# An attention kernel: GpSimd makes fraction and octave of VectorE's score tiles, and VectorE's cubic and last sum run on 16 bits

## The chip, the cores and the metric

The kernel runs on one core of a Trainium2 chip. The metric is the device time of one execution in microseconds; lower is better. The core's engines are TensorE (PE in the profile; its weight loads are PEld), VectorE (DVE), ScalarE (ACT), GpSimd (POOL) and SyncE (SP), which starts most of the DMAs.

## The reference

Two attention branches over the same input x (2048 tokens, width 512, 32 heads of 16) are mixed by a gate. Branch A is softmax attention; its scores are 32 heads x 2048 x 2048 exponentials, and they are nearly all of the work. Branch B is linear attention with a softmax feature map.

```python
g = sigmoid((x * gate_w).sum(-1, keepdims=True))
# A
q, k, v = heads(x @ A_wqkv)
p = softmax(einsum("bhqd,bhkd->bhqk", q, k) * 16 ** -0.5)
a = merge(einsum("bhqk,bhkd->bhqd", p, v)) @ A_wo
# B
q, k, v = heads(x @ B_wqkv)
pq, pk = q @ w_phi, k @ w_phi              # per head, 16 x 16
phi_q = concat(softmax(pq), softmax(-pq)); phi_k = concat(softmax(pk), softmax(-pk))
kv, z = einsum("bhsf,bhsd->bhfd", phi_k, v), phi_k.sum(tokens)
b = merge(phi_q @ kv / (phi_q @ z + 1e-6)) @ B_wo
return g * a + (1 - g) * b
```

## The kernel before

**Tiles.** A unit is one score tile, 128 keys x 512 queries of one head. There are 2048 of them. Four units, of four heads in four row groups of TensorE, make a pack; there are 512 packs, 16 (one for each block of 128 keys) to a group of four heads and one chunk of queries, and so 32 groups. TensorE writes scores to PSUM (L1076, `_scores`), an engine exponentiates them to SBUF, and TensorE multiplies with the values (L1203, `_values`). The denominator is a 17th column of ones in V.

**ScalarE's units.** Most units (`self.mine`) are exponentiated by ScalarE in groups of three and two tiles in turn (GROUPS), which use five PSUM banks as a ring (NRING): L1127, written to the ring ET of 25 slots. The other three banks go round among all other users (accumulators of A, projections, branch B, VectorE's scores).

**VectorE's units.** `_plan_vector` (L901) chooses the units in `self.away`: SHARES says how many for each of the 32 groups; they are spread over the places 1 to 14 of the 16 packs with an integer division. Four more are in SOON. Units are made in batches of five (NB), except FIRST (two batches of two), LAST (one of four) and an odd batch for what is left over. `_vector_batch` (L934) makes one batch:

- v_bits (L955, VectorE), one for each tile: the score in PSUM, scaled by log2(e), becomes a 32-bit fixed-point number in vt: the upper bits are the octave (the power of two), the lower ones the fraction.
- v_frac (L984, GpSimd, in `_frac`): the third byte of each 32-bit word, as a 16-bit float, to vf. In pieces of three and two tiles (PIECE = 3). In the SOON batches and the last two (TAIL) VectorE does it itself (L998).
- v_line, v_sq, v_cube (L1000 to L1002, VectorE): a cubic in the fraction, 16 bits, in vf and vu.
- v_out (L970, VectorE): the 32-bit word times 2^-17, plus the cubic, as an int16 in vu, whose bits are those of a bf16 exponential.

vt has two buffers (NVT), vf one, vu three (NVU). TensorE later takes the result as `pvx`.

**The order.** Nothing is scheduled on the chip: `Plan` holds every operation with an estimated cost, a due time (`prio`, in packs) and dependencies, and `order()` simulates the engines and writes out one fixed order for each, with semaphore waits. LEAD says how many packs ahead of its use a batch's scores are due, VPRIO, HURRY, EASE, QEASE, LEASE, OEASE and NUDGE move single due times. The names in PORT are those that share an SBUF port pair in the planner's model: a PORT operation of VectorE and an operation of GpSimd that is in PORT are never let run beside each other; each gets a dependency on the other's last one:

```python
            if o.port and e in port:
                other = port["DVE" if e == "POOL" else "POOL"]
                if other is not None:
                    o.deps.append(other)
                port[e] = o
```

TensorE's queue is in order. A `vqk` (scores of a VectorE unit) takes one of the three free banks and so waits until the bank's last user, often a v_bits, is done; the scores of ScalarE's next group stand behind it.

Branch B's work (`_b_part` L1354, keys early, queries in four parts later) and the normalisation of A (`_normed` L1249) run on VectorE in between; most of their operations are in PORT.

Of the kernel before, what the change touches and what calls it, by code (L numbers as in the profile page):

```python
# [10 lines left out]
P = 128  # L11
# [12 lines left out]
OCTAVE = 1.5 * 2.0 ** 30  # L24

# [10 lines left out]
class Job:  # L36


    def __init__(self):
        self.bank = None  # L40
        self.final = {}
        self.part = False


class Op:
    def __init__(self, eng, fn, cost, name, prio, rel, kind, lat, groups=None):
# [7 lines left out]
        self.acquire = None  # L54
        self.release = None
# [15 lines left out]
class Plan:  # L71
# [12 lines left out]
    PORT = {"v_frac", "v_line", "v_sq", "v_cube", "v_out", "gate_z", "gate_h", "gate_b", "n_den", "n_mul", "kvbd", "b_grid", "b_rest",  # L84
# [3 lines left out]
    def __init__(self):  # L88
        self.ops = []
        self.now = -1  # L90
        self.made, self.nudge = {}, {}
        self.free_banks = []
        self.loaded, self.turned = 0.0, False
        self.keep = None
        self.open = None
        self.pad = None
        self.live = False
# [41 lines left out]
    def _bank_for(self, o):  # L139

        return len(self.free_banks) > (self.keep is not None and self.keep is not o.acquire)
# [19 lines left out]
    def order(self):  # L161
# [17 lines left out]
        while left:  # L179
# [4 lines left out]
            for e in self.ENGS:  # L184
                found, limit = [], 1e9
                for o in avail[e]:
# [11 lines left out]
                    if o.acquire is not None:  # L198
                        if not self._bank_for(o):
                            continue  # L200
                        r = min(b[1] for b in self.free_banks)
                        if r > t:
                            t = r
# [85 lines left out]
            if o.acquire is not None:  # L289
                k = min(range(len(self.free_banks)), key=lambda i: self.free_banks[i][1])  # L290
# [3 lines left out]
            if o.release is not None:  # L294
                self.free_banks.append((o.release.bank, o.end + o.lat, [o]))
            if o.on_commit:
                o.on_commit(o)
# [94 lines left out]
class _Kernel:  # L392
# [5 lines left out]
    NB, NVU, LEAD = 5, 3, 13  # L398
    NVT, PIECE = 2, 3
    QDUE, VPRIO, VREL, TPRIO = 32.287, -12.758, 161.0, 1  # L400
# [9 lines left out]
    ENDS = 10  # L410
# [3 lines left out]
    REST = 53  # L414
    HURRY = (0.5, -7.6, 5.1, -6.5, 6.3, -11.8, 0, -8.0, 0, -17.8, -0.4, -1.2, -12.9, 25, 0, 8.1, 12.3, 0, 0.4, 10.0, 3.8, -1.8,
              -7.4, 0.7, 7.3, 25, 8.8, 25, 5.8, -6.9, 7.6, 3.4, -25, -14.5, 1.2, -7.3, -7.5, -20.6, -17.2, 21.6, -12.2, -4.6,
              0, 10.0, -0.9, -12.6, 11.2, -4.7, -4.7, 0.8, 0, 0, 0, 0, 0, 0, 0, 0, 0, 0)
    QEASE = (0, -10, -4.8, 6.8, 6.6, 10.5, 16, 11.0, -7.8, 7.8, -3.9, -6.4, -9.2, 10.5, 8.8, 16)
    LEASE = (-1.6, 3.6, 4.0, 0.7, -0.7, -14.9, 6.4, 16.5, -4.9, 3.4)
    OEASE = (11.6, 1.0, -4.4, 23.0, 18.8, 11.8, 17.2, 6.8, 5.3, -3.9, 1.0, 3.6, 8.7, 0, 0, 0)  # L420
    EASE = (-1.8, -6.9, 0, 0, 0, -0.2, 4.4, -4.4, 0.6, -6.3, 3.6, 0, 0, -14.4, -8.5, 1.4, -5.7, -1.4, -10.4, 0, -6.6, 5.8, 0,
              -4.2, -8.4, 7.4, -4.4, -6.5, 0, -5.6, 8.6, 2.8, -8.3, 10.0, 0, -4.3, 0, -5.7, -8.9, 0, 0, -1.5, -1.1, 5.6, 8.1,
              -3.6, 0, 7.0, -0.1, 0, 0, -4.5, -1.6, 0, 0, 4.2, 0, 0, 0, 0)
    NUDGE = {
        'b_max': {11: 3.7, 23: 22.2, 67: 10.7, 74: -19.5, 79: 13.2},
        'b_out': {3: 19.0, 11: 12.0, 17: 21.2},
        'b_part': {17: 21.2},
        'b_ratio': {2: -30.6},
        'b_rec': {8: 13.7},
        'b_slope': {6: -11.3},  # L430
        'b_square': {6: -16.5, 8: 11.6},
        'b_sum': {25: 27.1},
        'b_top': {7: -9.2, 9: 10.4},
        'bn_mul': {8: 43.5},
        'bv': {33: 6.1, 39: 10.5, 45: 19.5, 57: 8.1},
        'den': {13: 12.4},
        'kproj': {44: 0.8, 45: 6.5},
        'kproj_ev': {6: 7.4, 13: -15.7},
        'kv': {5: 11.6},
        'n_den': {9: -17.4},  # L440
        'n_mul': {10: 6.8, 14: 20.1},
        'n_rec': {3: 3.0},
        'n_t1': {20: 17.9, 26: 6.9},
        'num': {14: 12.6},
        'pq': {34: 13.8, 40: 29.9, 43: -1.4, 53: -11.9, 69: -25.9, 73: 8.8, 77: 14.1, 85: -7.9, 88: -0.9, 101: 13.5,
            120: 13.9},
        'pq_ev': {14: -22.9},
        'qproj_ev': {7: -7.8, 9: -10.7},
        'v_bits': {42: 17.3},
        'v_cube': {6: -3.1, 17: -11.8},  # L450
        'v_line': {10: 6.4, 46: -18.6},
        'vproj': {33: 3.1, 52: -14.5, 61: -3.2},
        'vproj_ev': {10: -13.3, 12: -7.6},
        'vqk': {75: 4.6, 78: -22.3, 124: 17.0, 130: -21.7, 149: 19.2, 156: 14.5},
# [440 lines left out]
    SHARES = (0, 2, 4, 6, 0, 5, 2, 8, 10, 5, 11, 10, 8, 8, 9, 12, 9, 10, 2, 9, 6, 11, 9, 14, 7, 10, 5, 13, 11, 7, 12, 9)  # L895
# [38 lines left out]
    def _vector_batch(self, number, units, due, step):  # L934
# [14 lines left out]
        parts = []  # L949
        for j, u in enumerate(units):  # L950
# [5 lines left out]
                vt[:, j, :], self._bank(job), SCALE * LOG2E * 2.0 ** 24, 2.0 ** 31,  # L956
# [6 lines left out]
        for name, cost, fn, reads, writes in self._cubic(flat(vt), flat(vf), flat(vu), n, b_vt, b_vf, b_vu):  # L963
# [6 lines left out]
        self.last_out = o = op("DVE", lambda e: e.scalar_tensor_tensor(  # L970
            out=flat(vu).bitcast(I16), in0=flat(vt), scalar=2.0 ** -17, in1=flat(vu), op0=ALU.mult, op1=ALU.add),
            self.c_dve(n), reads=[b_vt, b_vu], writes=[b_vu], name="v_out", prio=prio)
        if soon:
            self.b_bq[1][number].readers += b_vt.readers
        for j, u in enumerate(units):
            self.bits[u] = parts
            self.theirs[u] = (vu[:, j, :].bitcast(BF16), o, b_vu)

# [26 lines left out]
    def _attention(self):  # L1005
# [15 lines left out]
        a = 0  # L1021
        while a < len(self.mine):
            b = min(a + self.GROUPS[len(self.exps) % 2], len(self.mine))
# [4 lines left out]
            while len(self.pvs) < done // 4:  # L1028
                self._pv(len(self.pvs))
                if len(self.pvs) % (8 * NT) == 0:  # L1030
# [3 lines left out]
                    else:  # L1034
                        self.hooks.setdefault(int(self.Q0 + self.SQ * (4 * qc + 2)) + 10, []).append(
                            lambda qc=qc: self._out(qc))

# [55 lines left out]
    def _qk(self, a, b):  # L1093
        plan, NR = self.plan, self.NRING
        units = self.mine[a:b]

        def run(e):
            for _ in range(o.filled):
                e.matmul(self.ps[:, a % NR, :], self.kT[:, 0, 0:P], self.kT[:, 0, 0:QCH], start=True, stop=True)
            return self._scores(e, units, {u: self.ps[:, (a + k) % NR, :] for k, u in enumerate(units)})  # L1100
        k = len(self.qks)
        for x in range(a, b):
            self.in_group[x] = k
        o = plan.op("PE", run, self._wide(units[-1]), reads=self._score_bufs(units), name=f"qk{k}", prio=-1000, kind="row",
# [6 lines left out]
        o.on_commit = commit  # L1111
        o.pad = k >= 8
# [6 lines left out]
    def _exp(self, a, b):  # L1119
        plan, NR, NS = self.plan, self.NRING, self.NSLOT  # L1120
# [3 lines left out]
        for x in (a, b - 1):  # L1124
            if x >= NS:
                deps.append(self.pvs[self.mine[x - NS] // 4])
        o = plan.op("ACT", lambda e: e.activation(  # L1127
            self.ET[:, a % NS:a % NS + n, :], self.ps[:, a % NR:a % NR + n, :], ACT.Exp, scale=SCALE),
            self.c_act(512 * n), deps=deps, name=f"exp{k}", prio=self.mine[a] / 4 + 1)
        if a >= len(self.mine) - NR:  # L1130
            o.on_commit = lambda o: plan.free_banks.extend((x % NR, o.end + o.lat, [o]) for x in range(a, b))
# [561 lines left out]
```

## Time and profile before

| | |
|---|---|
| median of 3 runs | 828.64 us (828.54 to 829.0) |
| the profiled execution | 828.5 us, span 826.5 us |
| granted TensorE clock | 1.000 |
| PE / DVE / ACT / POOL busy | 789.5 / 781.7 / 816.3 / 127.4 us |
| first and last exponential group (L1127) | starts at 7.3 us and 820.3 us |
| exponential groups on ScalarE | 720 |
| v_bits on VectorE | 244 to vt and 4 (SOON) to bq |

The busy time of a group of instructions is the time in which at least one of them runs; the mean length of one is longer than its share of the busy time where neighbours overlap. "Idle before" is the time that the engine stood still just ahead of them, with what ended it. TensorE's busy time includes matmuls on zeros that the planner puts into gaps (L1212).

### The profile page before, as it was taken

The page shows a single profiled execution, that of the slowest core. Times are in us where ns is not written, and L with a number is a line of the kernel's source. Part 1 is how long each engine was busy: PE and PEld are TensorE (multiplying, and loading weights), DVE is VectorE, ACT ScalarE, POOL GpSimd, SP SyncE. Part 2 cuts the span into 40 slices and gives each one's busy share as a digit, 9 for nine tenths or more (in the row PEclk, how much of TensorE's full clock was granted, in tenths as well). Part 3 has the DMA queues.
Part 4 walks back from the last instruction along what each step waited for, and adds up shares of the span by engine and source line. Part 5 has one row for each costly group of instructions (what it writes and reads, how often), then busy time and mean ns, then how long its engine had stood idle before and what let it go on. Part 6 is the DMA issues. An engine that isn't in the chain of part 4 may idle for free.

```text
span 826.5 us, 19222 instructions
## 1 busy us (share of the span) xinstructions
PE 789.5 (96%) x8494; PEld 261.8 (32%) x8536; DVE 781.7 (95%) x1039; ACT 816.3 (99%) x725; POOL 127.4 (15%) x111
## 2 busy tenths in 40 slices
PE   9999999999999999999999999999999999999998
PEld 4323333333232222233222233222332222332344
DVE  6999999999999999999999999999999989999986
ACT  7999999999999999999999999999999999999997
POOL 3001100011012221012222011211122210122210
PEclk9999999999999999999999999999999999999999
DMA  9500000000000000030000031000320000310000
GB/s 233 177 7 8 1 5 4 1 8 3 1 8 2 1 8 1 9 71 14 2 7 1 21 59 28 12 2 6 52 39 21 2 1 21 65 27 8 2 2 27
DMA packets 49027, 19.99 MB, mean 24 GB/s; under 512 B 38704, under 2 KB 48944, under 8 KB 48944
## 3 DMA queue, kind: packets, MB, share of 16 engines
q1 hardware_dynamic: 48272, 18.58, 10.2%
q8 instruction: 66, 1.08, 0.5%
q10 hardware_dynamic: 672, 0.20, 0.1%
q14 instruction: 17, 0.14, 0.1%
HBM read 6.31 MB, written 2.10 MB: 10 GB/s over the span
## 4 chain that ended last, share of the span: by engine, by line
ACT 98%; PE 1%; DVE 0%; issue 0%
ACT ET L1127 98%; PE ps L704 0%; PE ps L786 0%; PE ps L723 0%; PE ps L1076 0%; PE ps L802 0%; DVE qT L813 0%; PE ps L1203 0%; DVE xT L735 0%; DVE xT L1641 0%; PE ps L1631 0%; DVE T L1256 0%; DVE onTA L1268 0%; DVE T L1264 0%; DVE rinv L1262 0%
## 5 line engine op out<-in xcount | busy, mean ns | idle before, releaser
L1127 ACT ACTIVATE ET<-ps 128x1536 bf16<-128x1536 f32 x720 | 814.0, 1389 | 0.6 <-PE ps L1076 0.5
L1076 PE MATMUL ps<-qT,kT 32*128 32x512 bf16 (+2 forms) x2248 | 318.8, 364 | 26.9 <-ACT ET L1127 16.7
L1212 PE MATMUL ps<-kT,zero 128*32 128x512 bf16 x2836 | 235.8, 384 | 0.1
L984 POOL TENSOR_SCALAR vf<-vt 128x1536 f16<-128x1536 uint8 (+1 forms) x96 | 118.9, 1253 | 648.4 <-DVE vu L970 350.3
L1203 PE MATMUL ps<-ET,V 128*32 128x512 bf16 (+2 forms) x1973 | 196.6, 364 | 0.7 <-ACT ET L1127 0.2
L1076 PEld LDWEIGHTS ps<-qT,kT 32*128 32x128 bf16 x2248 | 84.0, 91 | 303.3 <-ACT ET L1127 216.0
L955 DVE TENSOR_SCALAR vt<-ps 128x512 uint32<-128x512 f32 x244 | 159.0, 679 | 11.4 <-PE ps L1076 8.3
L970 DVE SCALAR_TENSOR_TENSOR vu<-vt,vu 128x2560 int16<-128x2560 uint32 (+3 forms) x51 | 137.7, 2700 | 0.5
L1212 PEld LDWEIGHTS ps<-kT,zero 128*32 128x32 bf16 x2836 | 61.8, 94 | 98.7 <-issue 77.8
L1203 PE MATMUL ps<-vu,V 128*32 128x512 bf16 (+1 forms) x275 | 90.1, 362 | 0.0
L1001 DVE TENSOR_TENSOR vf<-vf 128x2560 f16<-128x2560 f16 (+3 forms) x53 | 73.9, 1394 | 0.5
L1002 DVE TENSOR_TENSOR vu<-vu,vf 128x2560 f16<-128x2560 f16 (+3 forms) x53 | 73.8, 1393 | 0.4
L1203 PEld LDWEIGHTS ps<-ET,V 128*32 128x32 bf16 x1973 | 55.2, 95 | 58.6 <-issue 34.5
L752 PE MATMUL ps<-WB,xT 128*128 128x512 bf16 x164 | 47.9, 382 | 3.0 <-issue 1.3
L1000 DVE TENSOR_SCALAR vu<-vf 128x2560 f16<-128x2560 f16 (+3 forms) x53 | 41.0, 774 | 3.2 <-POOL vf L984 3.2
L752 PE MATMUL ps<-xT,WA 128*128 128x512 bf16 (+1 forms) x124 | 36.1, 380 | 0.4 <-DVE vt L955 0.4
L1203 PEld LDWEIGHTS ps<-vu,V 128*32 128x32 bf16 x275 | 24.6, 96 | 20.8 <-issue 13.9
L1256 DVE STREAM_TRANSPOSE T<-ps 128x512 f32<-128x512 f32 (+1 forms) x35 | 23.3, 666 | 5.1 <-PE ps L1203 4.8
L1367 DVE TENSOR_SCALAR bq<-ps 128x512 bf16<-128x512 f32 x32 | 21.3, 680 | 2.3 <-PE ps L752 2.3
L752 PEld LDWEIGHTS ps<-WB,xT 128*128 128x128 bf16 x192 | 14.1, 97 | 26.3 <-issue 14.3
L848 PE MATMUL ps<-WA,xT 128*128 128x128 bf16 x256 | 18.9, 220 | 0.2 <-issue 0.2
L1421 DVE TENSOR_TENSOR vt<-vt,brec 128x4096 bf16<-128x4096 bf16 (+1 forms) x10 | 18.6, 1859 | 0.1
(106 smaller groups left out, 424.8 us busy)
## 6 DMA issues: line engine op xcount, KB each, us to landing
qT<-qraw SPq DMA_DIRECT2D x120, 16.0 KB, 1.8
xn<-in_A_x_dram SPq DMA_DIRECT2D x3, 512.0 KB, 6.6
WB<-in_B_wqkv_dram SPq DMA_DIRECT2D x3, 512.0 KB, 5.4
out_dram<-WB SPq DMA_DIRECT2D x12, 128.0 KB, 1.8
WA<-in_A_wqkv_dram SPq DMA_DIRECT2D x3, 384.0 KB, 4.3
xn<-in_A_x_dram SPq DMA_DIRECT2D x2, 256.0 KB, 3.6
WoA<-in_A_wo_dram SPq DMA_DIRECT2D x1, 512.0 KB, 6.2
WoB<-in_B_wo_dram SPq DMA_DIRECT2D x1, 512.0 KB, 7.0
```

Source lines behind the costliest of these rows:

```text
L752: mm = op("PE", lambda e, c=c: e.matmul(self._bank(job)[:, 0:n], lhs(c), rhs(c), start=(c == 0), stop=(c == 3)), self.c_pe(n), reads=reads ...
L955: parts.append(op("DVE", lambda e, j=j, job=job: e.tensor_scalar(vt[:, j, :], self._bank(job), SCALE * LOG2E * 2.0 ** 24, 2.0 ** 31, op0=A ...
L970: self.last_out = o = op("DVE", lambda e: e.scalar_tensor_tensor(out=flat(vu).bitcast(I16), in0=flat(vt), scalar=2.0 ** -17, in1=flat(vu), ...
L984: "POOL", lambda e, a=at, n=n: e.tensor_scalar(vf[:, a:a + n, :], vt[:, a:a + n, :].bitcast(U8).rearrange("p n (q h) -> p n q h", h=4)[:, ...
L1000: lambda e: e.tensor_scalar(vu, vf, CUBE, SQUARE, op0=ALU.mult, op1=ALU.add), [b_vf], [b_vu]),
L1001: ("_sq", two, lambda e: e.tensor_tensor(vf, vf, vf, ALU.mult), [b_vf], [b_vf]),
L1002: ("_cube", two, lambda e: e.tensor_tensor(vu, vu, vf, ALU.mult), [b_vf, b_vu], [b_vu]),
L1076: ins = e.matmul(out[u][:, cols], self.kT[32 * i:32 * i + 32, cp, kt * TOK:(kt + 1) * TOK], self.qT[32 * i:32 * i + 32, s, q], start=True, ...
L1127: o = plan.op("ACT", lambda e: e.activation(self.ET[:, a % NS:a % NS + n, :], self.ps[:, a % NR:a % NR + n, :], ACT.Exp, scale=SCALE), sel ...
L1203: ins = e.matmul(self._bank(ot)[32 * i:32 * i + 32, to], self.V[:, kt, g8 // 2, v0:v0 + 32], tile[:, cols], start=first and j == 0, stop=o ...
L1212: ins = e.matmul(self._bank(ot)[32 * i:32 * i + 32, lo:QCH], self.zero[:], self.kT[:, 0, lo:QCH], start=False, stop=False, tile_position=( ...
L1256: return e.transpose(to, acc if alone else acc.rearrange("p (e b d) -> p e b d", e=2, b=8))
```

## The change

`_odd` is new and takes the place of `_frac`, `_cubic` and v_out in the batches that WHOLE marks (all but the SOON batches and the last two). In them the score is scaled so that the upper 16 bits of the word in vt are the octave and the lower 16 the fraction. GpSimd reads the lower halves and makes the fraction in vf (v_frac), and reads the upper halves and makes the int16 of the octave in vu (v_grid), both in pieces of two tiles. VectorE then computes an odd cubic, (THIRD v^2 + UNIT) v, in 16 bits, in the memory of vt itself, and v_out adds two 16-bit operands. v_grid is in PORT. Beside that, SHARES, LEAD, VPRIO, ENDS, REST and all due-time tables are new. Groups wider than three and two (WIDER) and reserved banks (`where`, `hold`, `booked`) are provided for; WIDER is all zero.

```diff
-    PORT = {"v_frac", "v_line", "v_sq", ...
+    PORT = {"v_frac", "v_grid", "v_line", "v_sq", ...
...
-    NB, NVU, LEAD = 5, 3, 13
-    NVT, PIECE = 2, 3
-    QDUE, VPRIO, VREL, TPRIO = 32.287, -12.758, 161.0, 1
+    NB, NVU, LEAD = 5, 3, 31
+    NVT, PIECE = 2, 2
+    QDUE, VPRIO, VREL, TPRIO = 32.287, -3, 161.0, 1
...
-    ENDS = 10
+    ENDS = 11
...
-    REST = 53
+    WHOLE = (1, 1, 1, ...
+    WIDER = (0, 0, 0, ...
+    LATER = 0.5
+    REST = 52
...
-    SHARES = (0, 2, 4, 6, 0, 5, 2, 8, 10, 5, 11, 10, 8, 8, 9, 12, 9, 10, 2, 9, 6, 11, 9, 14, 7, 10, 5, 13, 11, 7, 12, 9)
+    SHARES = (0, 2, 5, 4, 0, 4, 2, 10, 4, 12, 9, 9, 8, 7, 10, 15, 8, 10, 1, 8, 6, 11, 8, 13, 6, 11, 5, 13, 11, 8, 11, 11)
...
+        whole = not soon and len(self.batches) - self.TAIL > number and self.WHOLE[number]
+        scale, origin = (LOG2E * 2.0 ** 16, 127 * 2.0 ** 16) if whole else (LOG2E * 2.0 ** 24, 2.0 ** 31)
...
-                vt[:, j, :], self._bank(job), SCALE * LOG2E * 2.0 ** 24, 2.0 ** 31,
+                vt[:, j, :], self._bank(job), SCALE * scale, origin,
...
+        if whole:
+            self._odd(vt, vf, vu, n, parts, b_vt, b_vf, b_vu, prio)
...
+    def _odd(self, vt, vf, vu, n, parts, b_vt, b_vf, b_vu, prio):
+
+        halves = vt.bitcast(U16).rearrange("p n (q h) -> p n q h", h=2)
+        flat = lambda t: t.rearrange("p n q -> p (n q)")
+        power = flat(vt).bitcast(FP16)[:, 0:n]
+        v, out = flat(vf), flat(vu)
...
+        free, held, made, grid = b_vf.readers or b_vf.writers, b_vu.readers or b_vu.writers, [], []
+        for a, k in pieces:
+            made.append(self.plan.op("POOL", lambda e, a=a, k=k: e.tensor_scalar(
+                vf[:, a:a + k, :], halves[:, a:a + k, :, 0], 2.0 ** -16, SHIFT, op0=ALU.mult, op1=ALU.add),
+                0.165 + k * QCH * self.POOL, deps=[*parts[a:a + k], *free, self.last_out], name="v_frac", prio=prio))
+        for a, k in pieces:
+            grid.append(self.plan.op("POOL", lambda e, a=a, k=k: e.tensor_scalar(
+                vu[:, a:a + k, :].bitcast(I16), halves[:, a:a + k, :, 1], 128, BASE, op0=ALU.mult, op1=ALU.add),
+                0.165 + k * QCH * self.POOL, deps=[*parts[a:a + k], *held], name="v_grid", prio=prio + self.LATER))
+        b_vf.writers, b_vf.readers = made, []
+        b_vu.writers, b_vu.readers = grid, []
+        b_vt.readers += made + grid
+        two, four = 0.057 + n * 0.000525, 0.066 + n * 0.000262
+        op = lambda name, cost, fn, reads, writes: self.plan.op("DVE", fn, cost, reads=reads, writes=writes, name=name, prio=prio)
+        op("v_sq", two, lambda e: e.tensor_tensor(power, v, v, ALU.mult), [b_vf], [b_vt])
+        op("v_line", four, lambda e: e.tensor_scalar(power, power, THIRD, UNIT, op0=ALU.mult, op1=ALU.add), [b_vt], [b_vt])
+        b_vt.soon = [op("v_cube", two, lambda e: e.tensor_tensor(power, power, v, ALU.mult), [b_vt, b_vf], [b_vt])]
+        self.last_out = op("v_out", two, lambda e: e.tensor_tensor(out.bitcast(I16), out.bitcast(I16), power, ALU.add), [b_vt, b_vu], [b_vu])
```

184 lines of the change are left out of this document (122 added, 62 removed).

## The prediction

> **What bounds the kernel now.** I read the page's busy times and its chain first, then the groups by shape, the waits, the timeline of one batch, and last the groups in eight equal stretches of the span.
>
> ```profile
> PE 789.5 (96%) x8494; PEld 261.8 (32%) x8536; DVE 781.7 (95%) x1039; ACT 816.3 (99%) x725; POOL 127.4 (15%) x111
> ...
> ACT 98%; PE 1%; DVE 0%; issue 0%
> ...
> L1127 ACT ACTIVATE ET<-ps 128x1536 bf16<-128x1536 f32 x720 | 814.0, 1389 | 0.6 <-PE ps L1076 0.5
> ```
>
> The chain is ScalarE's exponentials from 8.9 us to 821.6 us, and their idle time is 0.6 us in all, 0.5 of it before the first. Around them lie 8.9 us of head, 4.9 us of tail and 2.0 us outside the span: the profiled execution took 828.5 us at a span of 826.5; the median of the runs is 828.64, 0.14 more. The two shapes of exponential, by form:
>
> ```profile
> L1127 ACT ACTIVATE ET<-ps 128x1536 bf16<-128x1536 f32 x360 | 576.5, 1601 | 0.5 <-PE ps L1076 0.5
> L1127 ACT ACTIVATE ET<-ps 128x1024 bf16<-128x1024 f32 x360 | 423.7, 1177 | 0.1
> ```
>
> They overlap, so their pace is not their length: 814.0/720 = 1.131 us a group on average, and 512 columns are 1601 - 1177 = 424 ns, so three tiles take 1.131 + 0.212 = 1.343 us of the engine and two take 0.919. One score tile more or fewer on ScalarE is about 0.45 us. The time is therefore the number of ScalarE's tiles, plus whatever ScalarE has to wait. VectorE takes 248 of the 2048 tiles; what that costs it and GpSimd (by form):
>
> ```profile
> L955 DVE TENSOR_SCALAR vt<-ps 128x512 uint32<-128x512 f32 x244 | 159.0, 679 | 11.4 <-PE ps L1076 8.3
> L970 DVE SCALAR_TENSOR_TENSOR vu<-vt,vu 128x2560 int16<-128x2560 uint32 x47 | 132.3, 2815 | 0.4
> L1001 DVE TENSOR_TENSOR vf<-vf 128x2560 f16<-128x2560 f16 x47 | 69.5, 1479 | 0.4
> L1002 DVE TENSOR_TENSOR vu<-vu,vf 128x2560 f16<-128x2560 f16 x47 | 69.5, 1479 | 0.3
> L1000 DVE TENSOR_SCALAR vu<-vf 128x2560 f16<-128x2560 f16 x47 | 38.4, 817 | 2.6 <-POOL vf L984 2.6
> ...
> L984 POOL TENSOR_SCALAR vf<-vt 128x1536 f16<-128x1536 uint8 x47 | 69.1, 1471 | 533.7 <-DVE vu L970 345.6 <-DVE bq L1438 120.5 <-DVE vt L955 67.5
> L984 POOL TENSOR_SCALAR vf<-vt 128x1024 f16<-128x1024 uint8 x49 | 51.2, 1045 | 114.7 <-DVE vt L955 110.0 <-DVE vu L970 4.7
> L645 POOL TENSOR_TENSOR wphi<-wphin,heads 128x512 bf16<-128x512 bf16 x1 | 1.1, 1051 | 1.7 <-DMA wphin<-in_B_w_phi_dram 1.7
> ```
>
> GpSimd is busy 15%, but not free: the planner lets no GpSimd fraction run beside a VectorE operation whose name is in PORT. The waits show both sides, and PE's room behind ScalarE:
>
> ```profile
> POOL vf L984 <- DVE vu L970: 350.3, 38, 20.4
> PEld ps L1076 <- ACT ET L1127: 216.0, 505, 0.9
> ...
> PEld ps L1076 <- DVE vt L955: 12.9, 35, 0.7
> ...
> DVE vu L1000 <- POOL vf L984: 3.2, 4, 1.8
> ```
>
> In 505 of 720 groups the scores wait for ScalarE, 0.43 us on average and 0.9 at most: TensorE can be that late before ScalarE idles.
>
> **The change, part by part.** *Tiles.* The new SHARES add up to 242, with SOON 246. Group 15 is given 15 tiles for the 14 places of its spacing rule, so that pack 248 comes twice: 246 tiles are computed on VectorE, 245 of them different. ScalarE is left 2048 - 245 = 1803 instead of 1800: 360 pairs of groups and one more group of three. That is +1.343 us on the path. Nothing hides it, as ScalarE has no idle time to give.
>
> *VectorE.* Batches of five fall from 47 to 46, the odd batch grows from one tile to four and stays, as TAIL has it, in the old form. In each five the last sum loses its 32-bit operand; the nearest rows are the two-input 16-bit ones of the same size, 1479 ns, so 2815 becomes 1479; square, line and cube keep 1479, 817 and 1479. The sum: 46 x 1.336 = 61.5 us saved, 1.1 on the two batches of two, 6.6 for the lost batch, 1.3 for two tiles of bits, less 4.4 for the grown batch: 781.7 becomes about 716 us. All of it lies beside ScalarE, so it is worth nothing in itself; it could only be spent on more tiles, and there are fewer.
>
> *GpSimd.* Each five had pieces of three and two (1471 + 1045 ns). It now has fractions of two, two and one, and as many octaves. Slope (1471 - 1045)/512 = 0.83 ns an element, so a piece of one is 0.62 us; six pieces are 2 x (1.045 + 1.045 + 0.62) = 5.42 us against 2.52. In all 188 pieces of two and 92 of one, 254 us for 119. The 16-bit input is read at the same spacing of 4 bytes as the byte before. No row shows an int16 result on GpSimd: bounds are the fraction's own 1045 ns for 1024 elements and the two-input row, 1051 ns for 512, or twice that. The lower end could lie below: the memset rows, 1259 ns for 1024 and 1805 for 2048, have a slope of 0.53. I take the fraction's, the one row with an operation of this form; anything faster changes nothing, for the floor is ScalarE's.
>
> *The order.* v_grid joins PORT, so VectorE's four operations (5.25 us a five) and GpSimd's six (5.42) exclude each other: 10.7 us, before 6.6 + 2.5 = 9.1. Under GpSimd only bits, evictions and transposes (319 us in all) may run. The square overwrites the bits and so waits for all six pieces, with every PORT operation behind it on VectorE. What a late VectorE holds up is a PSUM bank: TensorE's next vqk waits for it, and the scores stand behind that in TensorE's order. I sum PORT work by eighths of the span (101.6 us each), taking branch B's and the normalisation's PORT time from the rows of each stretch and 2.13 us for each new tile of its groups: 54, 84, 93, 108, 80, 103, 97 and 90 us. Handing over costs 0.25 us a batch, from this timeline (GpSimd starts 0.09 us after VectorE's end, VectorE 0.16 after GpSimd's):
>
> ```profile
> 402.23 2.78 DVE L970 SCALAR_TENSOR_TENSOR vu<-vt,vu 128x2560 int16<-128x2560 uint32 x1
> 405.12 2.70 DVE L955 TENSOR_SCALAR vt<-ps 128x512 uint32<-128x512 f32 x4
> 407.74 0.82 DVE L1000 TENSOR_SCALAR vu<-vf 128x2560 f16<-128x2560 f16 x1
> ...
> 405.10 2.48 POOL L984 TENSOR_SCALAR vf<-vt 128x1536 f16<-128x1536 uint8 x2 [7.97 <-DVE vu L970]
> ```
>
> So the fourth eighth (314 to 416 us, 8 batches) is overdrawn by 5.9 + 2.0 = 7.9 us and the sixth by 1.6 + 1.9 = 3.5. LEAD goes from 13 to 31 packs (a pack is 1.59 us), so the work may be done 49 us before its due time, as far as three buffers of results reach: the third eighth has 101.6 - 92.6 - 1.7 = 7.3 us to lend, the fifth 20. What is left uncovered is 7.9 - 7.3 = 0.6 us. [...]
>
> *Without effect.* WIDER is all zero, so no group becomes wider, the slots are those of before, and no bank is reserved. The duplicate tile costs VectorE, GpSimd and TensorE about 1.7, 1.1 and 0.4 us off the path. In the last group 11 tiles for 9 reach one pack nearer the end, still one before the last; the tail of 4.9 us is the normalisation and output of the last block and stays.
>
> The sum on the profiled execution: 828.5 + 1.34 + 0.6 = 830.4; on the median 830.6.
>
> **The rivals.**
> *ScalarE never waits (not slower by what can be told).* If pieces and lead fit with no uncovered time, only the extra group remains: 828.64 + 1.34 = 829.98, +0.16%. A measurement of this kernel can tell some 0.2% from no change, here 830.3, so this case counts as the same; it decides as long as new idle time on ScalarE stays under 0.3 us. For it: the kernel before has none over 814 us although VectorE waited up to 1.8 us for GpSimd. Against: there GpSimd had 15% and PORT work was never overdrawn.
> *The port becomes the bound in the dense stretches.* If three result buffers and one fraction buffer don't let work run ahead, the overdraft of 7.9 + 3.5 = 11.4 us reaches ScalarE in part or whole: 830.0 + 5.7 = 835.7 at half, 841 in full. It shows as VectorE waiting for GpSimd, and TensorE for v_bits. For it: from 212 us on the port is wanted for 570 + 11 us of 610. Against: averages leave room, and bits can run under GpSimd.
> *The octave is slow.* At the two-input row's rate a five costs 2.5 us more; the 43 fives' worth of tiles from 212 us on add 109 us to 581, 80 us past the 610 there: some 910 us. [...]
> *The edit is without its new path.* WHOLE is all ones, so all but the first two and last two batches take it; if they did not, the tiles alone would give 829.98 again; WHOLE gives that no chance worth a number.
>
> **How the numbers follow.** Forecast (830.3 to about 832, a handful of short stalls): 0.44. ScalarE never waits: 0.30. The port: 0.18. The slow octave: 0.07. A gain: 0.01, since the floor of 721 groups stands above the time before and only head or tail could give 3 us back. Slower by over 0.2%: 0.44 + 0.18 + 0.07 = 0.69; within: 0.30. The range runs from 829.7 (the floor, less the spread of the runs) to 835.7, half of the overdraft; above lie half the port case and the octave, 0.16 together.
>
> **What would show it.** 721 exponentials at an unchanged 1.131 us a group; L970's row gone for a two-input row of about 1479 ns; 280 pieces on GpSimd with 254 us; VectorE near 716 us; ScalarE's idle time between 0.6 and 2 us, its releaser TensorE's scores, mostly after 300 us. Wrong would be: octave rows far from 1045 ns, ScalarE's idle time spread evenly or many us, or under 721 groups.

## The result: 838.96 us, 1.2% slower than before, and the profile after

The changed kernel takes 838.96 us (median of 4 runs, 838.58 to 839.46), the kernel before 828.82 (828.54 to 829.61): a ratio of 1.0121 with a 95% interval of 1.0104 to 1.0139. The profiled execution of the changed kernel took 839.27 us at a span of 837.5. From its page, the busy times, the chain's shares by engine and the exponentials:

```profile
PE 799.9 (96%) x8610; PEld 265.5 (32%) x8653; DVE 723.1 (86%) x1033; ACT 822.3 (98%) x726; POOL 259.4 (31%) x295
...
DVE 37%; ACT 32%; POOL 18%; PE 9%; issue 2%; DMA 1%; SPq 0%; DVEq 0%
...
L1220 ACT ACTIVATE ET<-ps 128x1536 bf16<-128x1536 f32 x721 | 820.0, 1319 | 5.8 <-PE ps L1157 5.3
```

The chain was 98% ScalarE; now VectorE and GpSimd carry 55% of it, although VectorE is busy for less than before (723.1 us for 781.7) and GpSimd for only 31%. ScalarE's own row says what that costs. An exponential that starts late no longer overlaps the one ahead of it, so lost time shows in two columns, as idle time and as busy time with a shorter mean length (1319 ns for 1389). I therefore read busy and idle together. Before, 814.0 + 0.6 = 814.6; with one group more, 814.6 + 1.34 = 815.9; after, 820.0 + 5.8 = 825.8. ScalarE lost 9.9 us, of which 0.5 is a longer wait ahead of the first exponential, which starts at 7.35 us in both kernels and so costs nothing. The account of the two profiled executions: 828.5 + 1.34 (the group) + 9.2 to 9.4 (lost) + 0.42 (the tail, 5.33 us for 4.91) - 0.2 (outside the span, 1.8 for 2.0) = 839.3 to 839.5.

The same groups as before, by form; the columns are busy time, mean ns of one, idle time ahead with what ended it:

```profile
L978 DVE TENSOR_SCALAR vt<-ps 128x512 uint32<-128x512 f32 x242 | 155.9, 682 | 23.4 <-PE ps L1157 20.2
L1018 POOL TENSOR_SCALAR vf<-vt 128x1024 f16<-128x1024 uint16 x94 | 98.4, 1047 | 393.1 <-DVE vu L1033 226.0 <-DVE vt L978 131.6 <-DVE bq L1533 32.1
L1022 POOL TENSOR_SCALAR vu<-vt 128x1024 int16<-128x1024 uint16 x94 | 97.3, 1047 | 114.1 <-DVE vt L978 108.1 <-PE ps L1298 2.6
L1030 DVE TENSOR_TENSOR vt<-vf 128x2560 f16<-128x2560 f16 x46 | 68.3, 1485 | 30.7 <-POOL vu L1022 23.6 <-POOL vf L1018 7.1
L1032 DVE TENSOR_TENSOR vt<-vt,vf 128x2560 f16<-128x2560 f16 x46 | 68.2, 1483 | 0.6
L1033 DVE TENSOR_TENSOR vu<-vu,vt 128x2560 int16<-128x2560 int16 x46 | 68.0, 1479 | 0.7
L1031 DVE TENSOR_SCALAR vt<-vt 128x2560 f16<-128x2560 f16 x46 | 37.4, 813 | 1.2 <-POOL vu L1022 0.7
L1018 POOL TENSOR_SCALAR vf<-vt 128x512 f16<-128x512 uint16 x46 | 28.6, 621 | 3.6
L1022 POOL TENSOR_SCALAR vu<-vt 128x512 int16<-128x512 uint16 x46 | 28.5, 620 | 15.7 <-DVE vt L978 15.2
```

Every length is the one that was reckoned with: v_out 1479 ns, the octave as long as the fraction. But of two rows of equal length and count, the fraction is busy 98.4 us and the octave 97.3. The waits (us in total, times, longest):

```profile
PEld ps L1157 <- ACT ET L1220: 183.2, 429, 0.8
...
DVE vt L1030 <- POOL vu L1022: 23.9, 17, 2.5
PEld ps L1157 <- DVE vt L978: 22.1, 65, 0.7
PEld ps L1157 <- DVE vt L1032: 12.9, 26, 0.9
...
PEld ps L1298 <- DVE vu L1033: 6.1, 14, 0.9
ACT ET L1220 <- PE ps L1157: 5.3, 11, 1.0
```

This is the chain in numbers: the square (L1030) waits for GpSimd, TensorE's scores wait for v_bits and for the cube (before: 12.9 us in 35 waits and 4.5 in 12), and ScalarE for the scores. Only 429 groups find the scores waiting for ScalarE, where 505 did. The wait for the cube is written into the order: a vqk depends on the cube that last used the buffer of its bits. One such link, from the timeline: the cube ends at 348.8 us, TensorE's next scores wait 0.56 us for it, and the next group of exponentials comes 0.46 us late:

```profile
347.31 1.49 DVE L1032 TENSOR_TENSOR vt<-vt,vf 128x2560 f16<-128x2560 f16 x1
...
348.85 0.60 PE L1157 MATMUL ps<-qT,kT 32*128 32x512 bf16 x2 [0.56 <-DVE vt L1032]
...
350.57 2.37 ACT L1220 ACTIVATE ET<-ps 128x1024 bf16<-128x1024 f32 x2 [0.46 <-PE ps L1157]
```

GpSimd had idled 26 us by then; what reaches ScalarE here is VectorE's lateness from the batches ahead. In experiment 11 below, with the same order of work, this cube starts 3.05 us earlier, where ScalarE is 1.8 us earlier, and the group of exponentials does not wait.

The loss is spread: by eighths of the groups, from the ends of the exponentials beside those of the kernel before, 0.23, 0.53, 1.09, 1.41, 0.96, 1.13, 3.11 and 0.78 us. In the seventh, 1.6 us lie in one stretch with a halved clock. By windows of 1.7 us (length, PE, PEld, DVE, ACT and POOL busy, clock, DMA share, GB/s), after and then in the profiled run of experiment 4, whose instructions have the same order:

```profile
659.30:661.00 1.70, 0.95 (x8) 0.18 (x3) 1.70 (x3) 1.70 (x2) 0.71 (x1) 1.00 0.00 0
661.00:662.70 1.70, 1.31 (x17) 0.42 (x20) 1.70 (x4) 1.70 (x3) 1.54 (x3) 0.90 0.00 0
662.70:664.40 1.70, 1.70 (x17) 0.38 (x10) 1.70 (x2) 0.96 (x1) 0.46 (x1) 0.50 0.00 0
664.40:666.10 1.70, 1.64 (x7) 0.32 (x6) 0.98 (x2) 1.04 (x2) 0.32 (x1) 0.59 0.03 10
```

```profile
659.30:661.00 1.70, 0.92 (x7) 0.30 (x7) 1.70 (x4) 1.70 (x3) 1.25 (x2) 1.00 0.00 0
...
662.70:664.40 1.70, 1.54 (x11) 0.54 (x11) 1.70 (x2) 1.70 (x3) 0.25 (x1) 1.00 0.04 10
```

After the stretch in which TensorE was busy 0.95 us of 1.7, windows of 0.2 us show a granted clock of 0.50 from 662.4 to 665.6 us, 0.93 and 0.54 in the windows at its two ends and 1.00 outside, which makes 3.4 us at half, and ScalarE stood for 1.4 us (1.04 and 0.36 us ahead of two groups). In experiment 4 TensorE was as little busy (0.92) and the clock stayed at 1.00, so this part is not in every execution; what set the clock was not shown. What has to be explained in all of them is about 8 us.

**A spacing that the lengths hide.** The timeline of GpSimd shows three fractions of a batch of five and then three octaves (of the next batch: octaves mostly run one batch ahead, as they need not wait for vf):

```profile
265.80 2.87 POOL L1018 TENSOR_SCALAR vf<-vt 128x1024 f16<-128x1024 uint16 x3 [6.21 <-DVE vu L1033]
268.75 2.64 POOL L1022 TENSOR_SCALAR vu<-vt 128x1024 int16<-128x1024 uint16 x3
```

Pieces of the same lengths take 2.87 us as fractions and 2.64 as octaves. Octave follows octave 0.037 us before the end of the one ahead (1.010 us from start to start for two tiles), as the fractions of the kernel before did (1.434 us for 1471 ns). A piece that follows a fraction starts 0.079 us after its end (1.126 us), and so does a fraction that follows an octave: it is enough that one of the two neighbours is a fraction. I call these early and held. The hold is 0.116 us a piece; some 136 pieces are held, which makes 15.8 us of GpSimd's time, all of it while the planner lets no PORT operation of VectorE run. The order was written with 0.165 + 1024 x 0.00084 = 1.025 us for such a piece. The reported lengths do not tell the two apart: 1047 ns in both rows, with 1.010 or 1.126 us from start to start.

### The profile page after: what moved, and what is told of

The parts are those of the page before. It is cut to its first block, busy times and chain, and to the rows that moved or that the text cites. A ratio compares the mean times of both kernels' runs of the same rounds, so it can differ in the third digit from the quotient of the medians.

```text
span 837.5 us, 19640 instructions
## 1 busy us (share of the span) xinstructions
PE 799.9 (96%) x8610; PEld 265.5 (32%) x8653; DVE 723.1 (86%) x1033; ACT 822.3 (98%) x726; POOL 259.4 (31%) x295
## 4 chain that ended last, share of the span: by engine, by line
DVE 37%; ACT 32%; POOL 18%; PE 9%; issue 2%; DMA 1%; SPq 0%; DVEq 0%
ACT ET L1220 32%; POOL vu L1022 9%; POOL vf L1018 9%; DVE vt L1032 6%; DVE vu L1033 6%; DVE vt L1030 6%; PE ps L1157 3%; DVE vt L1031 3%; DVE vt L978 2%; PE ps L1307 2%; PE ps L1298 1%; DVE vt L1516 1%; DVE bq L1510 1%; DVE bq L1506 1%; DVE T L1359 1%
## 5 line engine op out<-in xcount | busy, mean ns | idle before, releaser
L1220 ACT ACTIVATE ET<-ps 128x1536 bf16<-128x1536 f32 x721 | 820.0, 1319 | 5.8 <-PE ps L1157 5.3
L1157 PE MATMUL ps<-qT,kT 32*128 32x512 bf16 (+2 forms) x2249 | 322.9, 365 | 23.4 <-ACT ET L1220 10.7
L1018 POOL TENSOR_SCALAR vf<-vt 128x1024 f16<-128x1024 uint16 (+1 forms) x140 | 127.0, 907 | 396.8 <-DVE vu L1033 226.0
L1307 PE MATMUL ps<-kT,zero 128*32 128x512 bf16 x2952 | 246.5, 384 | 0.0
L1022 POOL TENSOR_SCALAR vu<-vt 128x1024 int16<-128x1024 uint16 (+1 forms) x140 | 124.3, 907 | 129.8 <-DVE vt L978 123.2
L1307 PEld LDWEIGHTS ps<-kT,zero 128*32 128x32 bf16 x2952 | 65.2, 95 | 100.2 <-issue 77.0
L1030 DVE TENSOR_TENSOR vt<-vf 128x2560 f16<-128x2560 f16 (+1 forms) x48 | 69.7, 1452 | 31.0 <-POOL vu L1022 23.9
L1033 DVE TENSOR_TENSOR vu<-vu,vt 128x2560 int16<-128x2560 int16 (+1 forms) x48 | 69.4, 1446 | 2.3 <-POOL vu L1022 1.6
L1032 DVE TENSOR_TENSOR vt<-vt,vf 128x2560 f16<-128x2560 f16 (+1 forms) x48 | 69.6, 1450 | 0.7
L1031 DVE TENSOR_SCALAR vt<-vt 128x2560 f16<-128x2560 f16 (+1 forms) x48 | 38.2, 797 | 1.2 <-POOL vu L1022 0.7
```

What stands on the lines that cost most here:

```text
L1018: made.append(self.plan.op("POOL", lambda e, a=a, k=k: e.tensor_scalar(vf[:, a:a + k, :], halves[:, a:a + k, :, 0], 2.0 ** -16, SHIFT, op0 ...
L1022: grid.append(self.plan.op("POOL", lambda e, a=a, k=k: e.tensor_scalar(vu[:, a:a + k, :].bitcast(I16), halves[:, a:a + k, :, 1], 128, BASE ...
L1030: op("v_sq", two, lambda e: e.tensor_tensor(power, v, v, ALU.mult), [b_vf], [b_vt])
L1031: op("v_line", four, lambda e: e.tensor_scalar(power, power, THIRD, UNIT, op0=ALU.mult, op1=ALU.add), [b_vt], [b_vt])
L1032: b_vt.soon = [op("v_cube", two, lambda e: e.tensor_tensor(power, power, v, ALU.mult), [b_vt, b_vf], [b_vt])]
L1033: self.last_out = op("v_out", two, lambda e: e.tensor_tensor(out.bitcast(I16), out.bitcast(I16), power, ALU.add), [b_vt, b_vu], [b_vu])
```

## The experiments

The theories when they began: A, the held pieces break an order that has no room; B, the sheer amount of GpSimd and port work; C, something else in TensorE's order. The edits of the changed kernel (1 to 4, 6, 7, 9 to 11) leave the planner's costs as they are, so their instructions keep its order. "Lost" is busy and idle time of the exponentials over 815.9 us (after: 9.9).

**1. The fraction from one byte.** GpSimd reads the upper byte of the lower half, as the fraction of the kernel before read a byte.

```diff
-vf[:, a:a + k, :], halves[:, a:a + k, :, 0], 2.0 ** -16, SHIFT
+vf[:, a:a + k, :], byte[:, a:a + k, :], 1 / 256, SHIFT + 1 / 512
```

> The order of every engine is that of the changed kernel; only GpSimd's fraction is read as one byte (the upper byte of the lower half, times 1/256) instead of 16 bits, as the kernel before read it. Theory A (the spacing): in the trace of the changed kernel a piece of the 16-bit fraction holds back the next piece on GpSimd: pieces of two follow each other at 1.126 us where two octaves follow at 1.010, and the planner's order reckons 1.025; some 100 such pairs overdraw the port by 10 to 12 us and most of the 9 us that ScalarE loses comes from that. The byte fraction was followed 0.04 us before its end in the kernel before (1.434 us for 1471 ns), so the spacing should fall to 1.01 and the time to 830.5 to 832.5 us. Theory B (the port is overdrawn by its sheer load, 5% of GpSimd's time matters by 5%): 838 us at the least saving, 836 at best. Theory C (TensorE's own order, its filling matmuls or its clock): 838.5 to 839.5, unchanged.

840.28 us (837.84 to 841.51), ratio 1.0134 (1.0112 to 1.0155), lost 10.9 in the profiled execution, whose granted clock was 0.996. The fractions were still held: their row is busy 126.7 us for 140 pieces of 905 ns on average, the full sum of their lengths, where the early octaves' row, of the same lengths, is busy 124.1. So the 16-bit source is not what holds them, and A was not put to the test.

**2. Four forms by turns.** Destination and source of both operations change from batch to batch.

```diff
-vf[:, a:a + k, :], halves[:, a:a + k, :, 0], 2.0 ** -16, SHIFT
+vf[:, a:a + k, :].bitcast((FP16, I16, BF16, FP16)[form]), byte[:, a:a + k, :] if form == 3 else halves[:, a:a + k, :, 0],
+1 / 256 if form == 3 else 2.0 ** -16, SHIFT
-vu[:, a:a + k, :].bitcast(I16), halves[:, a:a + k, :, 1], 128, BASE
+vu[:, a:a + k, :].bitcast((I16, I16, FP16, I16)[form]), byte[:, a:a + k, :] if form == 3 else halves[:, a:a + k, :, 1],
+(128, 128, 16, 32)[form], BASE
```

> One look at spacings, by batches in turn of four forms, the order unchanged: fraction 16 bits to fp16 (as it is), to int16, to bf16, and byte to fp16; octave to int16 three times in four (the last of them from a byte) and to fp16 in the third form. The values are left wrong in three of four. Theory A1 (a 16-bit word read to a float is what holds the next piece back): spacing of pieces of two 1.126 us for fp16 and bf16 results, octaves to fp16 included, 1.010 for the int16 ones and for the byte. Theory A2 (it is the fraction's scalars, not the types): 1.126 for all fractions but the byte, 1.010 for all octaves, fp16 included. Theory A3 (it is the place or the buffer vf): 1.126 for all fractions, the byte too.

842.23 us (one run), lost 12.0. Fractions were held in every form, to int16 too (busy 126.7 us for 140 pieces of 905 ns, so none overlaps); octaves to int16 were early, from a half or a byte; the octave to fp16, which also had other scalars, was held (the octaves' row is busy 124.9 us, 0.8 more than in experiment 1, where all octaves were early). The types alone do not sort them.

**3. Hardly any octave.** From the sixth batch on, 16 of 512 columns.

```diff
+w = QCH if number < 5 else 16
-vu[:, a:a + k, :].bitcast(I16), halves[:, a:a + k, :, 1]
+vu[:, a:a + k, 0:w].bitcast(I16), halves[:, a:a + k, 0:w, 1]
```

> The order is that of the changed kernel; from the sixth batch of the new form on GpSimd makes only 16 of the 512 octaves of each tile, which leaves the rest of that work out: GpSimd loses some 115 us of its 254, the fraction stays as it is. Theories A and B (the port): ScalarE loses nothing beyond the extra group, 829.7 to 830.5 us. Theory C (TensorE): unchanged, above 837. If GpSimd's fraction alone (the wait of the next batch's fraction for the last sum) sets the pace: 833 to 837.

831.55 us (830.91 to 832.18), ratio 1.0031 (1.002 to 1.0041), lost 1.0, POOL busy 172.1 us. So the loss comes from GpSimd's work on the octaves, and C falls. A and B both remain.

**6. A shorter octave.** The octave leaves out 70 of 512 columns from the sixth batch on: 0.83 ns x 140 = 0.116 us for two tiles, the hold's own size. (Experiments 4 and 5 follow.)

```diff
+w = QCH if number < 5 else QCH - 70
-vu[:, a:a + k, :].bitcast(I16), halves[:, a:a + k, :, 1]
+vu[:, a:a + k, 0:w].bitcast(I16), halves[:, a:a + k, 0:w, 1]
```

> The order is that of the changed kernel; from the sixth batch of the new form on GpSimd makes 442 of the 512 octaves of each tile and leaves the other 70 out: a piece of two is 0.116 us shorter, a piece of one 0.058, some 12 us in all of GpSimd's 254, as much as the unreckoned spacing behind the fractions takes. Theory A (the order is built on a port with no room, and only the 10 to 12 us by which GpSimd's spacing exceeds what the planner reckons are lost): most of the 9 us come back, 830.5 to 832.5 us, ScalarE's lost time 1 to 2 us. Theory B (sheer load; 5% of GpSimd's time is worth 5% of the loss): 838 to 839. Theory C (TensorE): 838.5 to 840.

831.5 us (831.23 to 832.45), ratio 1.0034 (1.0022 to 1.0047), lost 1.4:

```profile
L1222 ACT ACTIVATE ET<-ps 128x1536 bf16<-128x1536 f32 x721 | 816.5, 1387 | 0.8 <-PE ps L1159 0.5
```

This is as little as without nearly all of the octave. 0.116 us a piece decides the time; leaving out the rest of the octave as well gains nothing. B falls.

**4. Scalars of the octave as floats.** In the source 128 and -68 are whole numbers.

```diff
-128, BASE
+128.0, float(BASE)
```

> The octave's two scalars are floating-point numbers (128.0 and -68.0) instead of whole numbers; values, types and order are those of the changed kernel. If GpSimd holds back a piece when it changes between operations with whole and with floating-point scalars, or because both are in the program, all pieces now follow each other 0.04 us before the end of the one before, pieces of two at 1.010 us, and by theory A the time falls to 830.5 to 832.5 us. If operations with floating-point scalars are always followed 0.08 us after their end, the octaves' spacing rises to 1.126 too, 10 us more of the port are gone, and the time is 843 to 848 us by theory A. If scalars have no part in it, spacings and 838 to 840 us stay.

838.09 us (837.81 to 842.11), ratio 1.0124 (1.01 to 1.0148), lost 8.0, spacings unchanged: fractions busy 126.6 us for 140 of 904 ns, octaves 124.0.

**5. The kernel before with pieces of two.**

```diff
-    NVT, PIECE = 2, 3
+    NVT, PIECE = 2, 2
```

> The kernel before with fractions in pieces of two, two and one instead of three and two. The order is a new one, with due times not fitted to it, so the time (840 to 850 us) says nothing; one look at the spacing on GpSimd, where no octave is made. If the hold is a matter of the pieces' size: 1.126 us between pieces of two. If it comes with the octaves in the program: 1.010.

846.58 us (one run), but of another order: the planner writes it anew, and TensorE's values become what ScalarE waits for (12.3 of 16.0 us); I did not follow that up. The spacing is what counts here, from its timeline of GpSimd:

```profile
305.11 2.63 POOL L984 TENSOR_SCALAR vf<-vt 128x1024 f16<-128x1024 uint8 x3 [7.47 <-DVE vu L970]
```

2.63 us for three fractions: early. The size of the pieces does not hold them.

**7. No whole scalars at all.**

```diff
-128, BASE
+128.0, BASE + 0.01
```

> The order is that of the changed kernel; the octave's added constant is -67.99 instead of -68, so that GpSimd gets a number that isn't whole (the result is rounded to the same int16). In the runs so far the pieces with whole scalars and an int16 result followed each other 0.04 us before the end of the one before, and every piece beside one of another kind 0.08 us after it, while in a program without octaves the fractions too came 0.04 us early. If it is the mixture in the program that holds the pieces back, all pieces now come early, 1.010 us for two tiles, and by theory A (the order has no room for more than 1.025) the 9 us of ScalarE shrink to 1: 830.3 to 831.7 us. If the hold belongs to scalars that aren't whole as soon as there is a second kind of operation, octaves are held too: some 100 more pairs by 0.116 us, and by theory A 842 to 848 us. By theory C nothing: 838 to 840.

838.25 us (837.32 to 842.13), ratio 1.0128 (1.0105 to 1.0152), lost 7.8; octaves early, fractions held (busy 124.0 and 126.6 us for 140 of 904 ns each). Whole or not is not it.

**8. One int16 operation in the kernel before.** A second kind of operation on GpSimd, 16 elements, at the start.

```diff
+self.mix = sb("mix", [P, 16], I16)
+op("POOL", lambda e: e.tensor_scalar(self.mix[:], self.iden[:, 0:16].bitcast(U16), 128, -68, op0=ALU.mult, op1=ALU.add), 0.2,
+   reads=[self.b_iden], name="mix", prio=-10)
```

> The kernel before with one more GpSimd operation at its start, 16 elements with whole scalars and an int16 result, which nothing uses; the order is otherwise the same. If the presence of a second kind in the program is enough for the hold, the fractions of three and two tiles come 1.55 us apart instead of 1.434, 47 times; the port there has room, and the time rises by 0 to 1.5 us (828.6 to 830.3). If only neighbours matter, spacing 1.434 and 828.5 to 829.3 us.

828.63 us (828.38 to 829.23), ratio 1.0003 (0.9993 to 1.0012), fractions still early (busy 118.9 us, as in the kernel before, for 96 of 1254 ns, 120.4 in sum). That two kinds of operation are mixed is not it.

**9. Holding the octave too.** It is written as fp16 with 16 and -68, the one form of octave that experiment 2 found held.

```diff
-vu[:, a:a + k, :].bitcast(I16), halves[:, a:a + k, :, 1], 128, BASE
+vu[:, a:a + k, :], halves[:, a:a + k, :, 1], 16, BASE
```

> The dose the other way: the octave's result is written as fp16 (16 times the octave) instead of int16, which leaves its values wrong; order and everything else are those of the changed kernel. In the look at forms such pieces followed each other 0.08 us after the end, as the fractions do. Theory A (no room on the port beyond what the planner reckons): some 80 more pairs by 0.116 us, 9 us more of port time, of which ScalarE loses nearly all: 844 to 848 us. Theory B (sheer load): 3.5% more GpSimd time, 839 to 840. Theory C (TensorE): 838 to 840.

846.09 us (845.05 to 847.71), ratio 1.0216 (1.0199 to 1.0233). The row of the exponentials gives 15.6 us lost, and the timeline shows both rows held:

```profile
L1220 ACT ACTIVATE ET<-ps 128x1536 bf16<-128x1536 f32 x721 | 823.2, 1302 | 8.3 <-PE ps L1157 6.3
```

```profile
266.53 2.87 POOL L1018 TENSOR_SCALAR vf<-vt 128x1024 f16<-128x1024 uint16 x3 [6.21 <-DVE vu L1033]
269.48 2.86 POOL L1022 TENSOR_SCALAR vu<-vt 128x1024 f16<-128x1024 uint16 x3
```

More pieces held, more time lost: the loss follows the hold in the other direction too.

**10. Scalars exchanged.** By turns of three batches.

```diff
-vf[:, a:a + k, :], halves[:, a:a + k, :, 0], 2.0 ** -16, SHIFT
+vf[:, a:a + k, :].bitcast((FP16, FP16, I16)[form]), (byte[:, a:a + k, :], halves[:, a:a + k, :, 0], halves[:, a:a + k, :, 1])[form],
+(1 / 256, 2.0 ** -16, 128)[form], (ROOT, 2.0, BASE)[form]
-128, BASE
+(128, 1.0, 2.0 ** -16)[form], (BASE, 0.5, SHIFT)[form]
```

> One look at spacings in three forms by turns, order unchanged, values left wrong in all: (a) the fraction as the kernel before had it, a byte times 1/256 plus 648.5/256; (b) the 16-bit fraction plus 2.0, and the octave with the scalars 1.0 and 0.5; (c) the octave's own operation written to vf, and the fraction's scalars (2^-16, 0.965) on the octave written to vu as int16. If the added scalar decides: (a) or (b) come 0.04 us before the end. If the destination decides: all to vf late, all to vu early. If scalars and result type decide together: (c) early in vf and late in vu.

831.77 us (one run), lost 2.3. All forms were early but one, the octave with the fraction's scalars. The timeline shows, in this order, the second form's fraction (2^-16 and 2.0), the third form's octave with the fraction's scalars, and the octave's operation at the fraction's place, with its int16 result. The octaves run a batch ahead, so those behind the second form's fractions are of the third; experiment 2 shows the same by its types, where octaves from a byte follow the fractions to bf16.

```profile
309.87 2.63 POOL L1021 TENSOR_SCALAR vf<-vt 128x1024 f16<-128x1024 uint16 x3 [6.00 <-DVE vu L1038]
312.59 2.87 POOL L1026 TENSOR_SCALAR vu<-vt 128x1024 int16<-128x1024 uint16 x3
321.45 2.63 POOL L1021 TENSOR_SCALAR vf<-vt 128x1024 int16<-128x1024 uint16 x3 [6.00 <-DVE vu L1038]
```

The hold moved with 2^-16 and 0.9649 to the octave's source, place and int16 destination, and left the place of the fraction. For this pair the scalars decide.

**11. The same mathematics with another pair.** The fraction is made larger by 2/0.964905, so that its second scalar is 2.0, and the cubic's coefficients take that back.

```diff
-SHIFT, THIRD, UNIT, BASE = 0.96490500, 9.99302049, 61.15905525, -68
+SIZE = 2.0 / 0.96490500
+SHIFT, THIRD, UNIT, BASE = 2.0, 9.99302049 / SIZE ** 3, 61.15905525 / SIZE, -68
-halves[:, a:a + k, :, 0], 2.0 ** -16, SHIFT
+halves[:, a:a + k, :, 0], SIZE * 2.0 ** -16, SHIFT
```

> The changed kernel in the same order with the same mathematics: the fraction's pair of scalars is scaled so that the added one is 2.0 instead of 0.9649 (both times 2.0728), and the cubic's two constants are scaled back. In the looks at forms the pair (2^-16, 2.0) came 0.04 us before the end of the piece before, (2^-16, 0.9649) 0.08 us after it, whatever types and places. If the pair of scalars decides and the added one is what counts, all pieces of GpSimd come early, and by theory A the 9 us that ScalarE loses shrink to about 1: 830.5 to 831.8 us. If it is the multiplier that counts or a rule that these two don't show, spacing 1.126 and 837.5 to 840 stay. Theory C: unchanged.

831.05 us (8 runs, 830.68 to 832.4) beside 828.46, ratio 1.0029 (1.0019 to 1.004), lost 1.2. The page's chain and exponentials, the waits, and the fractions of the batch shown above:

```profile
ACT 91%; DVE 4%; PE 2%; POOL 1%; DMA 1%; issue 0%; SPq 0%; DVEq 0%
...
L1221 ACT ACTIVATE ET<-ps 128x1536 bf16<-128x1536 f32 x721 | 816.0, 1387 | 1.1 <-PE ps L1158 1.1
```

```profile
PEld ps L1158 <- ACT ET L1221: 205.7, 483, 0.8
...
PEld ps L1158 <- DVE vt L979: 16.8, 51, 0.5
...
PEld ps L1158 <- DVE vt L1033: 3.7, 10, 0.5
```

```profile
264.37 2.63 POOL L1019 TENSOR_SCALAR vf<-vt 128x1024 f16<-128x1024 uint16 x3 [6.20 <-DVE vu L1034]
```

With 2.63 us for 2.87 the chain is ScalarE's again and TensorE waits 3.7 us for the cube where it waited 12.9. The new constants give back three quarters of the 10.1 us. What is left, 831.05 - 828.46 = 2.6, is the extra group (1.34), about 0.9 lost after the first exponential, and 0.4 in the tail.

**12. The held pair in the kernel before.**

```diff
-1 / 256, ROOT,
+1 / 256, 0.964905,
```

> The kernel before, in its own order, with 0.9649 in place of 2.5332 as the fraction's added scalar, which leaves its values wrong. If the scalars alone make the hold, without any octave in the program, the pieces of three and two come 1.55 us apart instead of 1.434. There the port is wanted for less than its time, so by theory A the 5 us more of it cost 0 to 1.5: 828.4 to 830. If GpSimd's spacing cost ScalarE time by itself, some 4 us: 832 to 833.

828.97 us (827.96 to 830.08), ratio 1.0003 (0.9994 to 1.0012). The timelines of a batch, this kernel's and then that of the kernel before:

```profile
372.42 2.59 POOL L984 TENSOR_SCALAR vf<-vt 128x1536 f16<-128x1536 uint8 x2 [9.07 <-DVE vu L970]
```

```profile
372.01 2.48 POOL L984 TENSOR_SCALAR vf<-vt 128x1536 f16<-128x1536 uint8 x2 [9.18 <-DVE vu L970]
```

The same hold, and no cost: GpSimd idles 9 us ahead of a batch there, and the exponentials' idle time stays 0.6 us. It costs only where the order has no room for it.

**The loss against the hold,** all in the changed kernel's order:

| kernel | pieces held | hold, 0.116 us each | lost |
|---|---|---|---|
| 11 | 0 | 0 | 1.2 |
| 10 (one run) | some 40 | 4.6 | 2.3 |
| 6 (octaves shorter by as much) | 136 | 15.8 | 1.4 |
| after; 1; 4; 7 | 136 | 15.8 | 9.9; 10.9; 8.0; 7.8 |
| 2 (one run) | some 156 | 18 | 12.0 |
| 9 | some 216 | 25 | 15.6 |

The loss over that of 11 is a quarter of a microsecond for each us of hold at the smallest dose and some half at the others (6.6 to 9.7 for 15.8, 10.8 for 18, 14.4 for 25). The profiled executions of the changed kernel and of 1 and 2 have a lower granted clock over the span (0.998, 0.996 and 0.996), which counts in their losses.

## Why the prediction was wrong

It said 830.6 us and at most 835.7; it was 838.96. The direction was right, the size was not.

**Right, by its own steps.** The extra group: 721 exponentials, and in experiment 11 the pace is back. VectorE: 723.1 us for 716, with v_out at 1479 ns. GpSimd: 280 pieces, 98.4 + 97.3 + 28.6 + 28.5 = 253 us for 254. The octave is as fast as the fraction, so that rival falls: 1024 elements take 1047 ns as an octave too, and the octave's two rows have a slope of (1047 - 620)/512 = 0.83 ns an element, the one that the prediction took from the fraction.

**The step that failed** is "What is left uncovered is 7.9 - 7.3 = 0.6 us". It was 9. Two things were wrong in it. The term that was mis-sized is the six pieces' 5.42 us: a sum of lengths, which leaves out how pieces follow each other. With fractions held, a five takes 2.87 + 0.08 + 2.64 = 5.59 us; with all early, 5.23 by the same rows; the order itself reckons with 2 x (1.025 + 1.025 + 0.595) = 5.29. And the balance by eighths was the wrong test. Against 5.42 the excess is only 0.17 us a five, 1.4 us in the eight batches of the fourth eighth, which makes 2 us uncovered, not 9. But the order is fixed for 5.29. The 0.30 us a five over that, 14 us in all, comes late into an order where the square, the bank and the scores are queued behind it, and more than half of it reaches ScalarE, also where the balance has room: 0.96 us in the fifth eighth, which had 20 us to lend and in which experiment 11 loses 0.00. (The first two eighths, with few batches, lose 0.23 and 0.53, and 0.07 and 0.25 in experiment 11.) That work which could have been done earlier is not, because nothing moves once the order is written, is my reading of this; whether the lateness passes through the square's own wait or through the other PORT operations queued behind GpSimd was not separated.

**The rivals.** The port rival, with 835.7 at half of its overdraft and 841 in full, named the right chain (VectorE waiting for GpSimd, TensorE for v_bits) and covers the time, but not for its reason: with the same instructions and dependencies, and in experiment 11 the same bytes, experiments 6 and 11 take 831 us. An overdraft of that size was not there; there was a hold on each piece that the order had not counted. It had 0.18. The exclusion that it and the sum by eighths rest on is the planner's, by the dependencies that it writes for the names in PORT; every kernel here has it, so what such operations of VectorE and GpSimd would cost each other side by side was not shown. "ScalarE never waits" (829.98) is not met even without the hold: 0.9 us stay lost in experiment 11.

**Smaller misses.** The tail was to stay at 4.9 us and is 5.33: VectorE's last evictions are now one of 512 columns and one of 256 (1.02 us together) where one of 256 (0.42 us) stood. The forecast's own signs said "ScalarE's idle time spread evenly or many us" would prove it wrong, and that is what the page shows. The longest wait of VectorE for GpSimd in the kernel before was 2.1 us (ahead of L1406), not the 1.8 that the prediction names. And a hand-over costs half of the 0.25 us a batch that were reckoned: where the two wait for each other in the changed kernel, GpSimd starts 0.083 us after VectorE's end and VectorE 0.034 us after GpSimd's; in the prediction's timeline VectorE was still busy with bits (until 407.82 us) when GpSimd ended.

**What stays open:** why a pair of scalars holds its own piece and the next. Early were (1/256, 2.533), (2^-16, 2.0), (2.07 x 2^-16, 2.0), (128, -68), (128, -67.99), (32, -68) and (1.0, 0.5); held were (2^-16, 0.9649), (1/256, 0.9669), (1/256, 0.9649), and (16, -68) to fp16. I know no rule that sorts them. The last differs from the early octaves in its destination and its multiplier at once, and no run separates the two. And none of these kernels beats the one before: with the hold gone the change still pays for the extra group, and whether the time freed on VectorE (723 us for 782) can carry more than 248 tiles was not tried.

## What to carry to other kernels

Take the price of a GpSimd piece from the spacing of starts of consecutive pieces in the same operation with the same constants, not from the mean length: here 1.010 and 1.126 us had one length. Where an order is fixed ahead and keeps the work of two engines apart, an uncounted tenth of a microsecond for each piece can reach the critical engine although the average of the stretch leaves room, as in the changed kernel, or cost nothing, as in experiment 12; compare the spacing with the cost that the order was written with before asking whether the average leaves room. A constant can be moved into a later operation at no cost where that operation has constants of its own, as in experiment 11, where VectorE's line took 797 ns on average with either pair.

## What the runs showed of the hardware

- The spacing of GpSimd's tensor_scalar pieces in these kernels went with the pairs of scalars of both neighbours: 0.036 us before the end of the piece ahead where both are early, 0.079 us after it where one is held. With (2^-16, 0.9649) neither the source (lower or upper half) nor the destination (fp16, bf16 or int16) changed it: 2.87 us for three pieces in the changed kernel and, from the upper half to int16, in experiment 10, and no overlap in the 126.7 us of experiment 2. The size of the pieces did not change it in either case: early 2.48 us for 1536 and 1024 elements and 2.63 for 1024, 1024 and 512, held 2.59 and 2.87.
- The reported length does not show it: 1045 to 1047 ns for 1024 elements in the kernel before, the changed one and experiment 11, 618 to 621 for 512 in the last two, and 904 or 905 on average over both sizes in experiments 1, 2, 4, 5, 7, 9 and 10.
- The granted clock of TensorE was 0.50 for 3.4 us in one execution in the changed order, after a stretch with 0.95 us of 1.7 busy, and 1.00 over the whole span of another (experiment 4) with 0.92 of 1.7. What decides between the two was not shown.
